# Forming the mixing's sums and differences in PSUM, with the softmax sums on ScalarE

## The chip, the core and the metric

The kernel runs on one core of a Trainium2 chip. The metric is the time of one launch on the device, in microseconds (us). A core has engines that each work through a queue of their own, in order: TensorE (PE in the profile, PEld its weight loads), VectorE (DVE), ScalarE (ACT), GpSimd (POOL) and SyncE (SP, which here only issues DMAs). TensorE writes into PSUM, eight banks of 512 fp32 columns on 128 partitions; VectorE and ScalarE read from there. Engines wait for one another through semaphores.

## The reference

Attention in two forms, the sum of which is mixed by a Fourier transform over positions and channels, and then goes through a feed-forward network. All is fp32; 8 batches, 8 heads, 576 positions, head size 64, 512 channels, 2048 hidden.

```python
out_d  = sm_attn(mean4(q), mean4(k), mean4(v))          # pooled by 4 positions
out_up = np.repeat(out_d, 4, axis=2)
scores = np.where(abs(i - j) < 4, scale * q @ k.T, -1e9)  # local, 7 positions wide
attn   = np.exp(scores - max); attn = attn / (np.sum(attn, axis=-1) + 1e-09)
x      = merge_heads(out_up + attn @ v)
...
mixed  = np.real(np.fft.fft(np.fft.fft(x, axis=1), axis=2))
u      = x + mixed
un     = (u - mean(u)) / np.sqrt(var(u) + 1e-06)
return u + np.maximum(un @ w_ch1, 0.0) @ w_ch2
```

## The kernel before

**Stages.** The work of the 8 batches runs in a pipeline. Up to about 270 us it is attention and mixing; the feed-forward network's first matmuls stand at about 271 us, the last mixing at about 320, and from 560 us on the network runs in a form with fewer products (`Super`). The weights arrive as 64-bit words and are decoded on the way (`Quarter`: ScalarE, GpSimd, three steps on VectorE, then a high and a low part).

**Attention.** A `Unit` is one of 40 spans of 128 positions of a batch: loads of q and k (`load`) and of v with a column of ones (`load_v`), `sum_in` (sums for the pooled attention), `scores`, `maxima`, `exps`, `transpose_p`, `copy_p`, `values`, `result`. Since v has a column of ones, the product `values` leaves the softmax sum in column D of PSUM. `result` (line 808) adds 1e-9 to these sums on VectorE into `rs` (line 817), takes the reciprocal and multiplies. `Pooled` does the same for the pooled attention of a batch in three groups (`result`, lines 651 to 665, with `rsd`).

**Mixing.** `Mix` transforms a batch. VectorE and GpSimd form sums and differences that use the symmetries (`cross`, `channels`, `fold`), TensorE multiplies over positions (`sequence`, `sequence_z`), and then over channels, in slots: two of 128 rows for each batch, and a third of 68 rows for each second batch, 20 in all. For a slot, `mix(t, 0)` forms the even part in one PSUM bank: a product with signs (L945) and two fp32 products with the channel table `chan` (L949), 256 columns each. ScalarE copies it to SBUF (`even_out`, L956), which frees the bank. `mix(t, 1)` forms the odd part in another bank, with two more products of L949. `unfold(t, 0)` and `unfold(t, 1)` (L968) are VectorE instructions that write even + odd and even - odd, interleaving two halves of 256 columns, into the tile `o` (or `ends` for the 68-row slots). Then the bank is given back, and SyncE stores `o` to `um` in DRAM (`store_mixed`), from where the network's blocks load it.

**Order.** Nothing reorders at run time. `at()` gives each step a place from the table `TURNS`, one number for each call of each step, and the steps are emitted in the order of these places, so that one table sets the order on all engines and queues, and with it which PSUM bank a step gets. Where the table has no entry, a step goes by a time in the plan (most of `Super`). The small constant `bits` (identity and mask in bf16) is loaded first on SyncE's queue (line 507); the larger constants come by GpSimd's queue (`constants`, lines 845 to 847).

Of the kernel before, what the change touches and what calls it, by code (L numbers as in the profile page):

```python
# [8 lines left out]
F32 = mybir.dt.float32  # L9
# [18 lines left out]
        49, 124, 252, 388, 530, 652, 781, 917,  # L28
    ),
    "Pooled.copy_v": (  # L30
        51, 131, 256, 395, 535, 659, 789, 918,
    ),
    "Pooled.scores": (
        38, 30, 33, 138, 95, 104, 270, 210, 229, 394, 347, 367, 539, 489, 505, 672, 604, 605, 786, 749, 759,
        937, 864, 890,
    ),
    "Pooled.maxima": (
        54, 32, 36, 149, 98, 110, 275, 212, 234, 402, 356, 382, 545, 495, 511, 675, 608, 614, 796, 751, 761,
        945, 873, 895,
    ),  # L40
    "Pooled.exps": (
        64, 37, 44, 154, 107, 125, 280, 215, 242, 418, 372, 393, 552, 504, 531, 688, 613, 629, 797, 757, 773,
        950, 878, 914,
    ),
    "Pooled.transpose_p": (
        83, 39, 61, 179, 117, 135, 303, 224, 274, 424, 381, 408, 555, 521, 544, 707, 623, 681, 814, 763, 793,
        953, 881, 923,
    ),
    "Pooled.copy_p": (
        85, 41, 66, 183, 122, 146, 308, 233, 279, 437, 386, 413, 569, 529, 558, 718, 634, 683, 819, 768, 811,  # L50
        955, 886, 936,
    ),
    "Pooled.values": (
        92, 53, 80, 192, 132, 153, 312, 267, 287, 439, 403, 425, 581, 540, 559, 720, 668, 694, 837, 804, 822,
        957, 925, 949,
    ),
    "Pooled.result": (
        94, 59, 86, 193, 137, 160, 317, 269, 293, 449, 409, 430, 591, 546, 570, 722, 674, 705, 843, 815, 825,
        963, 939, 951,
    ),  # L60
    "Pooled.store": (
        88, 251, 328, 522, 656, 770, 938, 968,
    ),
    "Pooled.pack": (
        112, 209, 345, 462, 601, 726, 869, 975,
    ),
    "Mix.cross": (
# [3 lines left out]
    ),  # L71
    "Mix.channels": (
# [4 lines left out]
    ),  # L77
    "Mix.fold": (
# [4 lines left out]
    ),  # L83
    "Mix.split_z": (
        99, 141, 194, 254, 349, 377, 501, 499, 577, 654, 710, 798, 852, 909, 987, 999,
    ),
    "Mix.sequence_z": (
        159, 316, 433, 513, 702, 824, 964, 1029,
    ),
    "Mix.z_high": (  # L90
        173, 335, 447, 518, 711, 829, 981, 1034,
    ),
    "Mix.z_low": (
        199, 337, 463, 528, 714, 836, 1000, 1098,
    ),
    "Mix.sequence": (
        216, 200, 175, 181, 338, 336, 332, 319, 476, 483, 458, 459, 573, 578, 600, 599, 762, 745, 742, 736,
        875, 876, 847, 854, 1001, 1007, 990, 995, 1052, 1045, 1071, 1081,
    ),
    "Mix.sequence_out": (  # L100
        228, 190, 344, 342, 488, 469, 588, 606, 764, 747, 885, 855, 1021, 1008, 1066, 1108,
    ),
    "Mix.mix": (
        257, 307, 243, 311, 401, 419, 354, 359, 366, 450, 502, 498, 516, 571, 626, 648, 609, 642, 677, 682,
# [1617 lines left out]
```

## Time and profile before

| | us |
|---|---|
| median of 3 runs | 1082.76 |
| lowest and highest | 1081.66, 1085.46 |
| the profiled execution | 1078.42 |
| its span, first to last instruction | 1076.6 |
| TensorE busy (matmuls) | 1036.2 |
| VectorE busy | 640.1 |
| ScalarE busy | 389.7 |
| GpSimd busy | 328.7 |

The profile is of one execution. Busy time is the time in which at least one instruction of an engine runs. Matmuls are pipelined: one of 512 columns lasts some 0.39 us in the rows, while the next starts 0.23 us after it, so that an uninterrupted sequence shows as fully busy and a wait shows a little shorter than it is. Each fp32 product appears as two passes, and so two rows, of the same line; the one-pass form of the network's products (fp32r) as one. In a row of the timeline or of the groups, `banks<-chan,yf` means that tile `banks` is written from `chan` and `yf`, and brackets or the last field name the idle time of the engine before the instruction, and who ended it. Rows of waits give who waited for whom, the total in us, the number of times and the longest. The busy table by stretches gives, for each, the length, then busy us and instructions of PE, PEld, DVE, ACT and POOL, then the granted clock of TensorE as a share of full speed, the DMA share and GB/s.

### The profile page before, as it was taken

The numbers are of one execution on the slowest core, as the hardware profiler recorded it, in microseconds if no ns is written. First come the engines' busy times: TensorE is split into PE (matmuls) and PEld (weight loads), VectorE is DVE, ScalarE is ACT, GpSimd is POOL, SyncE is SP. The second block draws the span as 40 slices with busy tenths as digits, with TensorE's granted clock in tenths as the row PEclk, the third lists the DMA queues.
The fourth block names the chain that finished last, engine by engine and source line by source line (L and its number), as shares of the span: only waits on it lengthen the run. The fifth ranks groups of instructions, "written<-read, shape, count | busy, mean of one in ns | idle before, by whom it ended". The sixth has DMA issues, their size and how long they took to land.

```text
span 1076.6 us, 21807 instructions
## 1 busy us (share of the span) xinstructions
PE 1036.2 (96%) x8296; PEld 831.4 (77%) x8296; DVE 640.1 (59%) x1226; ACT 389.7 (36%) x1069; POOL 328.7 (31%) x486
## 2 busy tenths in 40 slices
PE   6899999999999999989998999999999999999998
PEld 4677767777877788878886888887788887888886
DVE  6999979889997884354354333564334465333332
ACT  6775667664443442122241111252111143111121
POOL 1222223224654556464641121253212033200000
PEclk9999999999999999999999999999999999999999
DMA  9567768865745554865836787946978643953242
GB/s 349 185 233 237 239 180 243 253 177 172 201 127 180 153 147 133 190 190 163 196 137 175 227 229 204 281 115 170 272 232 224 199 136 89 247 184 136 78 127 78
DMA packets 114400, 201.61 MB, mean 187 GB/s; under 512 B 13792, under 2 KB 30080, under 8 KB 114168
## 3 DMA queue, kind: packets, MB, share of 16 engines
q1 hardware_dynamic: 99752, 173.08, 48.4%
q0 software_dynamic: 14544, 27.15, 14.6%
q8 instruction: 65, 1.06, 0.4%
q14 instruction: 39, 0.32, 0.1%
HBM read 143.22 MB, written 56.43 MB: 185 GB/s over the span
## 4 chain that ended last, share of the span: by engine, by line
PE 71%; DVE 10%; DMA 9%; issue 4%; POOL 3%; SPq 1%; ACT 1%; DVEq 0%; ACTq 0%; POOLq 0%
PE banks L1348 20%; PE banks L1211 11%; PE banks L1209 11%; PE banks L1210 11%; PE banks L1189 9%; PE banks L909 3%; DMA qkT<-in_qk_dram 2%; DMA raw<-in_wq_dram 2%; DVE wt L478 1%; PE banks L1162 1%; PE banks L949 1%; DMA ux<-xb 1%; DMA ut<-um 1%; PE banks L800 1%; DMA um<-o 1%
## 5 line engine op out<-in xcount | busy, mean ns | idle before, releaser
L1209 PE MATMUL banks<-w2h,hh 128*128 128x512 f32 x576 | 228.5, 397 | 0.0
L1211 PE MATMUL banks<-w2h,hl 128*128 128x512 f32 x576 | 225.8, 392 | 2.0 <-DVE hl L1197 1.9
L1210 PE MATMUL banks<-w2l,hh 128*128 128x512 f32 x576 | 225.2, 391 | 0.0
L1193 ACT ACTIVATE hh<-row 128x512 fp32r<-128x512 f32 x72 | 45.6, 633 | 290.1 <-DVE row L1375 173.2
L1348 PE MATMUL banks<-w,w 128*128 128x512 f32 x576 | 144.9, 395 | 4.0 <-ACT raw L1368 4.0
L1189 PE MATMUL banks<-unT,w 128*128 128x512 f32 x576 | 138.2, 392 | 1.1 <-DVE ut L1214 1.1
L1348 PEld LDWEIGHTS banks<-w,w 128*128 128x128 f32 x576 | 109.0, 190 | 28.7 <-ACT raw L1368 4.9
L1211 PEld LDWEIGHTS banks<-w2h,hl 128*128 128x128 f32 x576 | 108.1, 188 | 27.0 <-DVE hl L1197 3.3
L1189 PEld LDWEIGHTS banks<-unT,w 128*128 128x128 f32 x576 | 107.9, 188 | 24.8 <-DVE ut L1214 1.5
L1210 PEld LDWEIGHTS banks<-w2l,hh 128*128 128x128 f32 x576 | 108.2, 188 | 22.6
L1209 PEld LDWEIGHTS banks<-w2h,hh 128*128 128x128 f32 x576 | 108.3, 188 | 22.5
L1197 DVE SCALAR_TENSOR_TENSOR hl<-row,hh 128x512 fp32r<-128x512 f32 x72 | 50.4, 700 | 114.7 <-ACT hh L1193 114.2
L1348 PE MATMUL banks<-unT,w 128*128 128x512 f32 x432 | 106.2, 390 | 2.4 <-DVE w L1375 2.4
L1348 PEld LDWEIGHTS banks<-unT,w 128*128 128x128 f32 x432 | 80.8, 188 | 20.5 <-DVE w L1375 3.7
L1375 DVE TENSOR_TENSOR w<-raw,banks 128x512 f32<-128x512 f32 x48 | 33.0, 688 | 66.2 <-PE banks L1348 64.4
L1197 DVE SCALAR_TENSOR_TENSOR hl<-banks,hh 128x512 fp32r<-128x512 f32 x48 | 32.9, 686 | 65.3 <-ACT hh L1193 62.6
L759 ACT ACTIVATE sb<-banks,mx 128x64 f32<-128x64 f32 x320 | 69.8, 329 | 3.1 <-PE banks L772 1.8
L909 PE MATMUL banks<-seq,f 128*128 128x290 f32 x256 | 67.2, 411 | 2.1 <-DVE xb L820 2.1
L1193 ACT ACTIVATE hh<-banks 128x512 fp32r<-128x512 f32 x48 | 28.5, 594 | 106.9 <-PE banks L1210 73.6
L1147 POOL TENSOR_TENSOR rstd<-rstd,mhalf 128x1 f32<-128x1 f32 x36 | 23.8, 662 | 124.6 <-DVE rstd L1146 124.6
L909 PEld LDWEIGHTS banks<-seq,f 128*128 128x128 f32 x256 | 47.1, 190 | 15.0 <-DVE xb L820 2.2
L1315 POOL TENSOR_TENSOR raw<-raw 128x256 f32<-128x256 f32 x48 | 39.5, 824 | 52.8 <-ACT raw L1268 47.5
(131 smaller groups left out, 1557.2 us busy)
## 6 DMA issues: line engine op xcount, KB each, us to landing
w<-ut SPq DMA_DIRECT2D x96, 256.0 KB
qkT<-in_qk_dram SPq DMA_DIRECT2D x40, 512.0 KB
w<-ub SPq DMA_DIRECT2D x72, 256.0 KB
raw<-in_wq_dram SPq DMA_DIRECT2D x64, 256.0 KB
uh<-w SPq DMA_DIRECT2D x42, 256.0 KB
vaug<-in_vw_dram SPq DMA_DIRECT2D x40, 260.0 KB
out_dram<-ut SPq DMA_DIRECT2D x36, 256.0 KB
um<-o SPq DMA_DIRECT2D x16, 512.0 KB
```

The source lines that it names most:

```text
L759: nc.scalar.activation(out=self.sb[:, hp, z], in_=self.sc[:, z, hp], func=AF.Exp, scale=0.125, bias=self.mx[:, z, hp : hp + 1],)
L909: nc.tensor.matmul(y, l, r, start=(i == 0), stop=(i == len(mms) - 1))
L1147: nc.gpsimd.tensor_tensor(out=rstd, in0=rstd, in1=mhalf, op=ALU.pow)
L1189: nc.tensor.matmul(hps, a[:, c, :], unT[:, x, c, :], start=(i == 0), stop=(i == len(mms) - 1))
L1193: nc.scalar.activation(out=hh, in_=self.hps[f], func=AF.Relu)
L1197: nc.vector.scalar_tensor_tensor(out=hl, in0=self.hps[f], scalar=0.0, in1=self.hh[f].bitcast(F32), op0=ALU.max, op1=ALU.subtract)
L1209: nc.tensor.matmul(acc, hh, w2h, start=start, stop=False)
L1210: nc.tensor.matmul(acc, hh, w2l, start=False, stop=False)
L1211: nc.tensor.matmul(acc, hl, w2h, start=False, stop=stop)
L1315: nc.gpsimd.tensor_tensor(out=out, in0=a, in1=b, op=op)
L1348: nc.tensor.matmul(self.ps[into], w[:, y, c, :], both[z][:, c, :], start=(start and i == 0), stop=(i == len(mms) - 1), skip_group_check=True)
L1375: nc.vector.tensor_add(out=out, in0=raws[a], in1=self.ps[x])
```

## The change

- **Mixing.** A slot has one bank. `mix(t, 0)` forms signs, even and odd products all in it, which gives even + odd. `unfold(t, 0)` copies it out on ScalarE, with the interleaving. `mix(t, 1)` then adds two more products with tables that hold minus twice the odd ones, into the same bank, which gives even - odd, and `unfold(t, 1)` copies that out and gives the bank back. `even_out` and its tile are gone. The table `chan` has six parts in place of four.
- **Softmax sums.** The addition of 1e-9 (4e-9 in the pooled attention) is a step of its own, `total`, an activation on ScalarE with a bias from the small tile `little`; `result` starts with the reciprocal.
- **Constants.** `bits` is loaded by ScalarE's queue.
- **Places.** `TURNS` has new numbers for every step (1999 steps with a place, 1955 before).

```diff
-        49, 124, 252, 388, 530, 652, 781, 917,
+        55, 124, 259, 401, 546, 672, 814, 952,
...
+    little = res.tile([P, 2], F32, name="little")
+    for i, x in enumerate((1e-9, 4e-9)):
+        nc.vector.memset(little[:, i : i + 1], x)
...
-    nc.sync.dma_start(out=bits.bitcast(F32), in_=c_bits)
+    nc.scalar.dma_start(out=bits.bitcast(F32), in_=c_bits)
...
+        def total(self, g):
+            rs = self.rs[g] = pd.tile([P, 2, 2], F32, name="rsd", bufs=2)[:, :, : self.tiles(g)]
+            nc.scalar.activation(out=rs, in_=self.av[g][:, :, :, D], func=AF.Identity, bias=little[:, 1:])
+
         def result(self, g):
-            av, k = self.av[g], self.tiles(g)
-            rs = pd.tile([P, 2, 2], F32, name="rsd", bufs=2)[:, :, :k]
-            nc.vector.tensor_scalar_add(out=rs, in0=av[:, :, :, D], scalar1=4e-9)
+            av, k, rs = self.av[g], self.tiles(g), self.rs[g]
             nc.vector.reciprocal(out=rs, in_=rs)
...
+        def total(self):
+            self.rs = p2.tile([P, 2, HP], F32, name="rs", bufs=2)
+            nc.scalar.activation(out=self.rs, in_=self.av[:, :, :, D], func=AF.Identity, bias=little[:, :1])
...
-            rs = p2.tile([P, 2, HP], F32, name="rs")
-            nc.vector.tensor_scalar_add(out=rs, in0=self.av[:, :, :, D], scalar1=1e-9)
+            rs = self.rs
             nc.vector.reciprocal(out=rs, in_=rs)
...
-    chanm = pf.tile([P, 4, HN], F32, name="chan")
+    chanm = pf.tile([P, 6, HN], F32, name="chan")
...
-        def mix(self, t, odd):
+        def mix(self, t, minus):
 
             cols = self.kept(t)
-            ps = self.ps[t, odd] = bank((self, t, odd), "mix", P if t < 2 else 2 * TAIL)[:, 0]
-            if not odd:
+            if not minus:
+                ps = self.ps[t] = bank((self, t), "mix", P if t < 2 else 2 * TAIL)[:, 0]
                 sg = signs.unsqueeze(2).to_broadcast([P, 2, HD])
                 to = ps.rearrange("p (two n) -> p two n", two=2)
                 nc.tensor.matmul(to, yz[:, cols], sg, start=True, stop=False, skip_group_check=True)
-
-            for half, T in enumerate((3, 1) if odd else (0, 2)):
+                parts = [(0, 0, 0), (1, 2, 2), (0, 3, 3), (1, 1, 1)]
+            else:
+                ps = self.ps[t]
+                parts = [(0, 3, 4), (1, 1, 5)]
+            for half, T, way in parts:
                 to = ps[:, half * HD : (half + 1) * HD]
                 nc.tensor.matmul(
-                    to, self.yh[:, T, cols], chanm[:, T, :], start=bool(odd), stop=True, skip_group_check=True
+                    to, self.yh[:, T, cols], chanm[:, way, :], start=False, stop=way > 2 or way == 1, skip_group_check=True
                 )
-
-        def even_out(self, t):
-            ps = self.ps[t, 0]
-            self.even[t] = pf.tile([P, DM], F32, name="even", bufs=2)[: ps.shape[0]]
-            nc.scalar.copy(out=self.even[t], in_=ps)
-            done((self, t, 0), "mix")
...
-            even, ps = (x.rearrange("p (two n) -> p n two", two=2) for x in (self.even[t], ps))
-            nc.vector.tensor_tensor(
-                out=o.rearrange("p (n two) -> p n two", two=2),
-                in0=even,
-                in1=ps,
-                op=ALU.subtract if minus else ALU.add,
+            nc.scalar.copy(
+                out=o.rearrange("p (n two) -> p n two", two=2), in_=ps.rearrange("p (two n) -> p n two", two=2)
             )
-            if len(self.mixed.setdefault(t, [])) == 1:
-                done((self, t, 1), "mix")
-            self.mixed[t].append(minus)
+            if minus:
+                done((self, t), "mix")
...
-    chan = np.stack([cos[:, 0::2], sin[:, 1::2], cos[:, 1::2], sin[:, 0::2]], axis=1)
+    chan = [cos[:, 0::2], sin[:, 1::2], cos[:, 1::2], sin[:, 0::2]]
+    chan = np.stack([*chan, -2 * chan[3], -2 * chan[1]], axis=1)
```

TensorE's order at the first mixing of a batch, before (L945 and L949 are the mixing's products with `signs` and `chan`, L740 scores, L567 and L642 pooled v and values, L593 and L623 pooled scores and transposes):

```order
L740 MATMUL banks<-qkT 64x64 x16
L567 MATMUL banks<-vaug,poolm 32x260 x8
L567 MATMUL banks<-vaug,poolm 64x260 x2
L945 MATMUL banks<-signs,yz 128x512
L949 MATMUL banks<-chan,yf 128x256 x2
L642 MATMUL banks<-vsum,ptd 64x65 x16
L593 MATMUL banks<-sums 32x160 x8
L623 MATMUL banks<-ident,sd 128x128 x6
```

The same place in the changed kernel (L958 and L965 are the mixing's products, L750 scores, L649 pooled values, L630 pooled transposes, L782 transposes):

```order
L750 MATMUL banks<-qkT 64x64 x16
L649 MATMUL banks<-vsum,ptd 64x65 x16
L958 MATMUL banks<-signs,yz 128x512
L965 MATMUL banks<-chan,yf 128x256 x6
L630 MATMUL banks<-ident,sd 128x128 x6
L965 MATMUL banks<-chan,yf 128x256 x2
L782 MATMUL banks<-ident,sb 128x128 x4
```

The six products of L965 are the first four of slot 0 and the second pair of slot 1, whose first four stand further up; slot 0's second pair follows the six transposes.

ScalarE's order at the mixing's first copies, before (L956 copies an even part, L755 and L759 are a unit's scaling and exps, L604 and L607 the pooled ones, L572 and L573 copy the pooled v):

```order
L607 ACTIVATE sd<-banks,mxd 128x5x32
L956 COPY even<-banks 128x512
L755 ACTIVATE mx<-mx 128x8
L759 ACTIVATE sb<-banks,mx 128x64 x8
L572 COPY vsum<-banks 128x520
L573 COPY vsum<-banks 128x260
L956 COPY even<-banks 128x512
```

And in the changed kernel (L977 copies out a sum or a difference, L660 adds to the pooled softmax sums, L765 and L769 are a unit's scaling and exps, L499 rounds a weight):

```order
L579 COPY vsum<-banks 128x520
L580 COPY vsum<-banks 128x260
L499 CAST w_156<-wt 128x256
L977 COPY o_1547<-banks 128x512
L765 ACTIVATE mx<-mx 128x8
L769 ACTIVATE sb<-banks,mx 128x64 x8
L660 ACTIVATE rsd<-banks,little 128x4
L977 COPY o_1547<-banks 128x512
L977 COPY o_1573<-banks 128x512
```

The first L977 is slot 1's sum, the second slot 0's, behind a unit's exps and a softmax sum, the third slot 1's difference.

SyncE's first DMAs, before (`vaug` is v, `qkT` is q and k, `raw` weights):

```order
L507 DMA bits<-in_c_bits_dram 128x96
L711 DMA vaug<-in_vw_dram 128x520 x2
L707 DMA qkT<-in_qk_dram 128x1024 x5
L711 DMA vaug<-in_vw_dram 128x520
L707 DMA qkT<-in_qk_dram 128x1024 x2
```

And in the changed kernel:

```order
L717 DMA qkT<-in_qk_dram 128x1024 x5
L721 DMA vaug<-in_vw_dram 128x520 x2
L717 DMA qkT<-in_qk_dram 128x1024
L721 DMA vaug<-in_vw_dram 128x520 x3
L717 DMA qkT<-in_qk_dram 128x1024 x3
```

`bits` has moved to the head of ScalarE's queue, and five loads of q and k stand ahead of the first v.

## Rows read from the trace of the kernel before

**Rows 1.** The profile's page: busy us, share and instructions of each engine

```profile
PE 1036.2 (96%) x8296; PEld 831.4 (77%) x8296; DVE 640.1 (59%) x1226; ACT 389.7 (36%) x1069; POOL 328.7 (31%) x486
```

**Rows 2.** Busy time by stretches: length, PE, PEld, DVE, ACT, POOL, clock, DMA

```profile
0.00:60.00 60.00, 46.33 (x1140) 35.30 (x1141) 47.83 (x97) 41.23 (x155) 12.12 (x31) 1.00 0.75 268
60.00:270.00 210.00, 201.75 (x3665) 152.52 (x3664) 190.30 (x426) 136.83 (x470) 60.31 (x105) 0.99 0.70 215
270.00:360.00 90.00, 85.18 (x374) 67.41 (x373) 77.19 (x154) 37.84 (x93) 51.14 (x82) 1.00 0.59 168
360.00:450.00 90.00, 90.00 (x398) 74.53 (x398) 55.59 (x100) 26.76 (x66) 51.69 (x75) 1.00 0.56 152
450.00:560.00 110.00, 106.91 (x492) 87.71 (x492) 50.69 (x86) 29.85 (x69) 57.80 (x78) 1.00 0.64 177
```

**Rows 3.** Who waited for whom, 0 to 60 us: total us, times, longest

```profile
PE banks L740 <- DMA qkT<-in_qk_dram: 3.1, 2, 2.5
...
PE banks L800 <- DVE odt L660: 2.5, 2, 2.3
...
PE banks L593 <- DVE odt L660: 1.4, 1, 1.4
...
PE banks L593 <- DVE rs L817: 0.9, 1, 0.9
```

**Rows 4.** The same, 60 to 270 us

```profile
PE banks L593 <- DVE xb L820: 2.1, 1, 2.1
PE banks L909 <- DVE xb L820: 2.1, 1, 2.1
...
PE banks L642 <- DVE yz L931: 0.5, 1, 0.5
```

**Rows 5.** The same, 270 to 360 us, and last 360 to 560 us

```profile
PE banks L1211 <- DVE hl L1197: 1.9, 2, 1.2
...
PE banks L949 <- DVE hl L1197: 0.7, 1, 0.7
...
PE banks L1162 <- DVE hl L1197: 3.1, 1, 3.1
```

**Rows 6.** Timeline of VectorE: start, us, instruction, idle before and who ended it

```profile
154.17 1.22 DVE L723 TENSOR_REDUCE sums<-qkT 128x256 f32<-128x1024 f32 x1 [3.18 <-DMA qkT<-in_qk_dram]
...
223.70 0.69 DVE L820 TENSOR_TENSOR xb<-banks,rs 128x512 f32<-128x512 f32 x1 [2.29 <-DMA ud<-rest]
...
462.03 3.15 DVE L1069 TENSOR_TENSOR raw<-w 128x512 f32<-128x512 f32 x2 [2.38 <-POOL wt L1079]
```

**Rows 7.** The chain that ended last, 340 to 357 us: start, us, what

```profile
337.18 4.62 DMA raw<-in_wq_dram
```

**Rows 8.** Groups by line: shapes, count, busy us, mean ns, idle before

```profile
L949 PE MATMUL banks<-chan,yf 128*128 128x256 f32 (+1 forms) x160 | 42.2, 390 | 0.7 <-DVE hl L1197 0.7
...
L968 DVE TENSOR_TENSOR o<-even,banks 128x512 f32<-128x512 f32 x32 | 21.5, 694 | 0.2
...
L956 ACT COPY even<-banks 128x512 f32<-128x512 f32 (+1 forms) x20 | 12.0, 598 | 7.8 <-PE banks L949 7.8
...
L755 ACT ACTIVATE mx<-mx 128x8 f32<-128x8 f32 x40 | 8.9, 223 | 19.2 <-DVE mx L752 18.9
...
L817 DVE TENSOR_SCALAR rs<-banks 128x8 f32<-128x8 f32 x40 | 6.3, 158 | 2.1 <-PE banks L800 1.9
...
L968 DVE TENSOR_TENSOR ends<-even,banks 68x512 f32<-68x512 f32 x8 | 5.2, 684 | 0.0
```

**Rows 9.** Timeline of ScalarE's first exps, TensorE's pooled transposes and channel products

```profile
9.26 1.75 ACT L759 ACTIVATE sb<-banks,mx 128x64 f32<-128x64 f32 x8
...
18.80 0.87 PE L623 MATMUL banks<-ident,sd 128*128 128x128 f32 x6 [0.34 <-ACT sd L607]
...
68.60 1.03 PE L949 MATMUL banks<-chan,yf 128*128 128x256 f32 x4
```

**Rows 10.** Timeline of TensorE at the start

```profile
7.07 1.13 PE L740 MATMUL banks<-qkT 64*64 64x64 f32 x32 [2.53 <-DMA qkT<-in_qk_dram]
```

More of the change, by code (lines that the diff above doesn't have):

```diff
@@ L52 @@
+        995, 929, 971,
     ),
     "Pooled.values": (
-        92, 53, 80, 192, 132, 153, 312, 267, 287, 439, 403, 425, 581, 540, 559, 720, 668, 694, 837, 804, 822,
-        957, 925, 949,
+        96, 59, 74, 210, 142, 175, 343, 270, 305, 484, 422, 441, 616, 564, 584, 752, 686, 720, 874, 827, 850,
+        1005, 964, 978,
+    ),
+    "Pooled.total": (
+        105, 64, 82, 211, 150, 178, 345, 280, 313, 487, 423, 444, 618, 581, 588, 755, 697, 730, 880, 843,
+        855, 1013, 972, 990,
     ),
@@ L116 @@
+        820, 833, 832, 853, 985, 1002, 965, 993, 946, 958, 1091, 1127, 1077, 1134, 1179, 1289, 1183, 1213,
+        1155, 1171,
     ),
     "Mix.store_mixed": (
-        357, 436, 624, 828, 904, 1058, 1152, 1267,
+        311, 440, 585, 750, 943, 1040, 1158, 1317,
     ),
     "Mix.store_local": (
-        115, 184, 273, 292, 389, 380, 512, 572, 671, 667, 784, 865, 922, 961, 996, 1004,
+        112, 219, 263, 314, 417, 408, 548, 597, 698, 741, 845, 861, 966, 948, 1051, 1055,
     ),
     "Mix.store_ends": (
-        562, 831, 1199, 1306,
+        473, 937, 1123, 1277,
@@ L157 @@
     ),
     "Unit.values": (
[L159 to L160 removed]
+        39, 78, 65, 87, 101, 131, 168, 201, 218, 241, 297, 319, 344, 358, 361, 437, 460, 489, 501, 508, 663,
+        605, 621, 633, 651, 740, 753, 786, 763, 776, 851, 883, 907, 932, 896, 984, 1017, 1027, 1011, 1037,
+    ),
+    "Unit.total": (
+        41, 89, 68, 99, 108, 136, 169, 204, 224, 247, 301, 320, 349, 360, 363, 438, 477, 494, 509, 512, 671,
+        611, 625, 644, 653, 747, 754, 787, 770, 781, 862, 885, 910, 934, 904, 992, 1034, 1029, 1015, 1045,
@@ L549, in __init__ @@
             self.b = b
-            self.sp, self.mx, self.tp, self.pt, self.av, self.rest = {}, {}, {}, {}, {}, None
+            self.sp, self.mx, self.tp, self.pt, self.av, self.rs, self.rest = {}, {}, {}, {}, {}, {}, None
         def pool_v(self):
@@ L689, in plan @@
             at(self.copy_v)
-            stages = [self.scores, self.maxima, self.exps, self.transpose_p, self.copy_p, self.values, self.result]
+            stages = [self.scores, self.maxima, self.exps, self.transpose_p, self.copy_p]
+            stages += [self.values, self.total, self.result]
             for g in (2, 0, 1):
@@ L829, in plan @@
                 *(self.load, self.sum_in, self.load_v, self.scores, self.maxima, self.exps),
-                *(self.transpose_p, self.copy_p, self.values, self.result),
+                *(self.transpose_p, self.copy_p, self.values, self.total, self.result),
             ):
@@ L853, in __init__ @@
             self.b, self.y = b, {}
-            self.w, self.ps, self.o, self.even, self.mixed = {}, {}, {}, {}, {}
+            self.w, self.ps, self.o = {}, {}, {}
             self.f = self.yh = self.ends = None
@@ L1021, in plan @@
             for slot in range(2 + self.b % 2):
-                at(self.mix, slot, 0)
-                at(self.even_out, slot)
-                at(self.mix, slot, 1)
                 for minus in range(2):
+                    at(self.mix, slot, minus)
                     at(self.unfold, slot, minus)
```

169 lines of the change are left out of this document (80 added, 89 removed), and 102 rows, old and new, of the table TURNS.

## The prediction

> **What bounds the kernel now.** I read the busy shares first. TensorE (PE) is busy for 96% of the span, VectorE (DVE) for 59%, ScalarE (ACT) for 36% [rows 1]. These averages hide two regimes, so I read the stretches next [rows 2]; look at PE and DVE side by side. From 360 to 450 us PE is busy for all 90 us, with 398 matmuls, 226 ns each, while DVE works 55.6 us: there PE alone sets the pace. From 60 to 270 us, where attention and mixing run, PE is busy for 201.75 of 210 us and DVE for 190.30: both are close to full. Work that goes from DVE to PE then pays only as far as PE's idle time is DVE's doing, so that idle time is the whole budget. Before 560 us it is 13.7 + 8.3 + 4.8 + 0 + 3.1 = 29.8 us, the length less PE's busy time in the five rows of [rows 2]. After 560 us the change touches nothing but places.
>
> Who ended those idle times is read from the waits [rows 3 to 5]. I sort them by what DVE itself was doing. In 0:60, 4.8 us are waits for DVE (2.5 + 1.4 + 0.9) and 3.1 for the first q and k loads [rows 3]. In 60:270 seven rows name DVE, from 2.1 down to 0.5 us, together 8.2 [rows 4]; but the two longest, 2.1 us each, aren't DVE's load: DVE had itself idled 3.18 us for a load and 2.29 us for a store [rows 6]. 4.0 us remain. In 270:360 all 4.7 us name DVE, in four rows from 1.9 down to 0.7 [rows 5]. About half, 2.3 us, stand behind transfers of raw weights that pace the decoding on DVE, such as the 4.62 us at 337 [rows 7]; 2.4 us remain. The 3.1 us of [rows 5] at 467 us follow a DVE that had waited 2.38 us for GpSimd (POOL) [rows 6]. So 4.8 + 3.1 + 4.0 + 2.4 = 14.3 us are within reach of lighter DVE queues and an earlier first load, 2.1 + 2.1 + 2.3 + 3.1 = 9.6 us were begun by transfers and POOL, and 5.9 us are the rest.
>
> **The change, part by part: PE.** The profile counts two passes for each fp32 product: L949 has 160 for 20 slots with four products each [rows 8]. The changed kernel has six for each slot, so 20 x 2 x 2 = 80 more passes. Four such passes start and end within 1.03 us, and one lasts 0.39 [rows 8, 9], so starts are (1.03 - 0.39) / 3 = 0.213 us apart. All have 256 moving columns, those of the 68-row slots too. The cost is 80 x 0.213 = 17 us. The signs product L945 stays as it is, and mixing goes on breaking PE's order twice for each slot. Nothing is taken off PE, and nothing can hide these passes except PE's own idle time.
>
> **DVE.** Removed are 40 combinations (21.5 + 5.2 us) and 64 additions to the softmax sums (158 ns each, 10.1 us) [rows 8], together 36.8 us; two memsets come in. Most, some 28 us, falls between 60 and 270 us, where attention runs and three quarters of the combinations stand. DVE then needs some 162 us where PE needs over 200: it is no longer PE's equal.
>
> **ACT.** Removed are 20 copies of even parts, 12.0 us [rows 8]. Added are 40 copies that interleave. ACT's price for the interleaved read isn't in the trace; between the plain copy, 598 ns, and DVE's combination with that pattern, 694 ns [rows 8], I take 0.6, the same engine's: 24 us, at most 28. The 64 sums are small ACT instructions; nearest is the scaling of the maxima, 223 ns for 128x8 [rows 8]: 14.3 us, bounds 13 and 20. Net +26 us. ACT's 136.8 of 210 us in 60:270 [rows 2] rise to some 156, three quarters. It is not full, but at that load others queue behind it.
>
> **The waits that come in.** Two are new. First, the second pair of products writes into the bank that the first copy reads, so PE must wait for that copy, and all that stands behind on PE waits too, scores and values of later units included. How thin the cover can be shows at the first such place in the order: between slot 0's first four products and its second pair, PE has slot 1's second pair (0.85 us) and six transposes (0.87 us [rows 9]); ACT has a scaling, eight exps, a sum and the copy, 0.22 + 1.75 + 0.22 + 0.6 = 2.8 us [rows 8, 9]. If both arrive together, PE waits 2.8 - 1.7 = 1.1 us. Of the other 19 slots, read in the same way, four or so have so little cover; the rest have scores, values or pooled products between. Second, each softmax sum goes PE, ACT, DVE and no longer PE, DVE. That costs PE nothing while banks are free: it holds a bank some 0.2 us longer, against the one bank that each slot of the mixing gives back.
>
> **Start and constants.** The small constant goes to ACT's queue; ACT's first exps stand at 9.26 us [rows 9], so its issue costs nothing there. On SyncE's queue (SP) five q and k loads now come first, where the constant and two loads of v did. The first product with q and k stands at 7.07 us behind its load [rows 10]. An earlier landing can give back between nothing (all transfers behind it still have to pass) and the 3.1 us of [rows 3]. Later on SP, the mixing's stores wait for ACT's copy in place of DVE's combination, and the q and k loads behind them with them. The larger channel table is one POOL DMA as before, long ahead of its first use at 68 us [rows 9].
>
> **The sum.** +17 us of PE work. Of the 14.3 us within reach I take three quarters, 10.7 us: where DVE is at 62% of a stretch (360:450) PE never waits, where it is at 86% (270:360) PE idles for 5% of it [rows 2], and DVE will stand at some 75%, between the two. The 9.6 us begun by transfers I leave. 17 - 10.7 = +6.3 us. The profiled execution took 1078.4 us, so its like would take 1084.7; the median of the three runs is 1082.8, so I predict 1082.8 + 6.3 = **1089 us**. For this kernel a difference under 0.3%, 3.25 us, can't be told from none.
>
> **A rule against this reading.** Between 60 and 270 us the weight loads are busy for 152.52 of 210 us, 73%; from 360 to 450, where PE is surely full, 74.53 of 90, 83% [rows 2]. The Trainium skill (Perfetto Trace Analysis, "Identifying the Most-Contended Engine") says that the busy share of matmuls is no good measure of how near TensorE is to its limit, and that the busy share of its weight loads is a better one. By that rule PE would have a tenth of those 210 us free, some 20 us, the added passes would cost next to nothing, and the relief alone would give 1082.8 - 10.7 = 1072. The idle times of the matmuls, 8.3 us there, don't bear that out, so it has part of the chance of the faster rival and no more.
>
> **Rivals.** *Faster, 1076.* The new places also move the loads and stores that began the long waits, and PE, no longer held by DVE, runs without those gaps: 14.3 + 9.6 = 23.9 us come back, 17 - 23.9 = -6.9 us. For it: 360:450 shows that PE can run so. Against it: it needs four fifths of PE's idle time before 560 us, and a wait for a transfer doesn't end because DVE is lighter. *The same, 1083.* All of the 14.3 and a third of the 9.6 come back: 17.5 against 17. For it: the order is written anew for the new loads. Against it: all engines share one order, and ACT is now fuller. *Slower by more, 1097.* ACT takes DVE's place as the engine that PE waits for: five thin covers at 1.1 us are 5.5 us, and a quarter of the relief, 2.7 us, is lost where sums stand behind exps: 6.3 + 5.5 + 2.7 = +14.5. It decides from the point at which ACT comes to a copy over 1.7 us after PE has finished the products it reads.
>
> **How the numbers follow.** The forecast around 1089 (1086 to 1093): 0.33. Slower by more, 1093 to 1102: 0.14. The same, 1079.5 to 1086: 0.26. Faster, below 1079.5: 0.27. So faster by over 0.3% has 0.27, within 0.3% 0.26, slower by over 0.3% 0.47. As the cases lie on both sides, the forecast's own range is 1086 to 1093; the range meant to hold the time 8 times in 10 goes from 1074 to 1098 and leaves out a full return of all waits and the worst of the ACT rival.
>
> **What would show it.** The channel products as 240 passes, their starts still 0.213 us apart, and PE's busy time up by some 17 us: that is the certain term. DVE's busy time in the first 270 us down by over 30 us. PE's idle time before 560 us at 18 to 20 us: that is the relief; near 6 us means the faster rival, near 28 the slower one. Waits of PE for the interleaving copy, by name, would show ACT's part. The first q and k product before 7.07 us would show the start. I am wrong if the added passes lie beside other work, so that PE's busy time hardly grows, or if the idle time after 560 us, which I carry over unchanged, moves by more than 3 us.

## The result and the profile after

| | before | changed |
|---|---|---|
| median, us | 1084.11 (4 runs) | 1096.38 (4 runs) |
| lowest and highest, us | 1081.66, 1085.64 | 1094.48, 1099.13 |
| profiled execution, us | 1078.42 | 1099.13 |
| its mean granted clock of TensorE | 0.997 | 0.986 |

The changed kernel is slower by 1.24% (ratio 1.0124, 95% interval 1.0098 to 1.0150), some 13 us. The forecast was 1089 and its range reached to 1098, so the sign and the range held, and the point is 7 us too low. The granted clock doesn't explain the difference: at a mean clock of 0.994 the changed kernel took 1094.48 us, and the kernel before, in the experiments below, 1079.7 to 1084.6. The two profiled executions lie below all timed runs of before and at the top of the changed kernel's, so the traces show a difference of 20.7 us, 8 us more than the medians.

The busy line of the page, against [rows 1]: TensorE +23.5 us, VectorE -39.9, ScalarE +23.1.

```profile
PE 1059.7 (97%) x8376; PEld 852.4 (78%) x8376; DVE 600.2 (55%) x1124; ACT 412.8 (38%) x1153; POOL 330.3 (30%) x486
```

The stretches of [rows 2] for the changed kernel (length, then busy us of PE, PEld, DVE, ACT, POOL, then clock, DMA share, GB/s):

```profile
0.00:60.00 60.00, 52.36 (x1198) 40.30 (x1199) 47.30 (x89) 46.87 (x181) 11.69 (x30) 0.94 0.80 287
60.00:270.00 210.00, 201.66 (x3625) 154.00 (x3625) 155.96 (x320) 148.00 (x515) 54.17 (x96) 0.98 0.66 200
270.00:360.00 90.00, 83.69 (x369) 65.44 (x366) 70.48 (x140) 38.20 (x91) 50.97 (x81) 0.98 0.63 174
360.00:450.00 90.00, 89.09 (x394) 73.47 (x393) 57.29 (x112) 28.53 (x71) 44.45 (x70) 1.00 0.55 155
450.00:560.00 110.00, 106.94 (x469) 87.52 (x468) 41.82 (x80) 23.44 (x53) 63.88 (x87) 0.97 0.61 156
```

Read PE and DVE side by side. DVE works 203.3 us in the first 270 us, where it worked 238.1. Part of these 35 us is only that the changed kernel is less far at 270 us: up to the network's first product after attention, at 274.94 us before and now at 291.07, DVE works 242.2 and 220.2 us, 22 us less. PE's idle time before 560 us is 7.6 + 8.3 + 6.3 + 0.9 + 3.1 = 26.2 us, where it was 29.8. Up to the first product of `Super`, which is the same work in both, the stretches are (before, then changed):

```profile
0.00:562.20 562.20, 532.36 (x6072) 419.25 (x6073) 422.06 (x860) 274.70 (x857) 234.75 (x373) 1.00 0.65 195
0.00:581.40 581.40, 555.14 (x6153) 438.47 (x6154) 382.11 (x756) 297.36 (x939) 236.30 (x373) 0.98 0.64 189
```

PE idles 29.8 us there before and 26.3 now (length less busy time), while DVE is 40 us lighter. Ten times as much was lifted off DVE as PE idles less.

Who is waited for has changed, though. Summed over all rows of TensorE's waits in these two stretches, waits for DVE fell from 21.7 to 12.2 us, by 9.5, and all others rose from 7.4 to 13.1, by 5.7: for transfers from 3.4 to 5.9, for ScalarE from 2.7 to 4.5, the rest from 1.3 to 2.7. Waits of TensorE from 60 to 270 us, against [rows 4]:

```profile
PE banks L574 <- DMA vaug<-in_vw_dram: 4.5, 1, 4.5
...
PE banks L810 <- DVE rs L831: 0.9, 1, 0.9
...
PE banks L922 <- DVE xb L833: 0.3, 1, 0.3
```

And from 270 to 360 us, against [rows 5]:

```profile
PE banks L965 <- ACT ends L977: 3.1, 1, 3.1
PE banks L1165 <- DVE un L1157: 1.3, 2, 0.9
PE banks L1214 <- DVE hl L1200: 0.9, 1, 0.9
```

From 60 to 270 us the waits for `xb` on DVE are 0.3 us, where they were 4.2, and one for `ends` on DVE is gone, which before had been:

```profile
PE banks L623 <- DVE ends L968: 1.3, 1, 1.3
```

In their place stand one wait of 4.5 us for a load of v and one of 3.1 us for a copy on ScalarE. In both cases what TensorE waits for stands behind other work in a queue. TensorE at the first of them (start, us, instruction, idle before):

```profile
233.97 1.10 PE L574 MATMUL banks<-vaug,poolm 128*32 128x260 f32 x12
239.58 2.15 PE L574 MATMUL banks<-vaug,poolm 128*32 128x260 f32 x8 [4.51 <-DMA vaug<-in_vw_dram]
```

SyncE at the same time:

```profile
228.96 0.90 SPq L987 DMA_DIRECT2D um<-o  x2
229.95 2.73 SPq L721 DMA_DIRECT2D vaug<-in_vw_dram  x1
232.77 5.42 SPq L1006 DMA_DIRECT2D ux<-xb  x4
```

The load stands behind the mixing's stores on SyncE's queue and is issued over 229.95 to 232.68, with more stores behind it; PE has come to the product that reads it by about 235. At the second, ScalarE has a weight ahead of the copy, and the weight's transfer is late:

```profile
297.69 1.07 ACT L469 ACTIVATE wt<-raw 128x256 f32<-128x256 f32 x3 [7.73 <-DMA raw<-in_wq_dram]
298.67 0.57 ACT L977 COPY ends<-banks 68x512 f32<-68x512 f32 x1
```

The groups of the edit, against [rows 8] (shapes, count, busy us, mean ns, idle before):

```profile
L965 PE MATMUL banks<-chan,yf 128*128 128x256 f32 (+1 forms) x240 | 60.0, 391 | 3.1 <-ACT ends L977 3.1
L977 ACT COPY o<-banks 128x512 f32<-128x512 f32 x32 | 18.8, 597 | 5.4 <-PE banks L965 5.3
```

The channel products are 240 passes and 17.8 us longer than the 42.2 of L949; the interleaving copy takes 597 ns.

### The profile page after: what moved, and what is told of

Same layout as the page of the kernel before. It is cut to its first block, busy times and chain, and to the rows that moved or that the text cites. A ratio compares the mean times of both kernels' runs of the same rounds, so it can differ in the third digit from the quotient of the medians.

```text
span 1097.4 us, 21962 instructions
## 1 busy us (share of the span) xinstructions
PE 1059.7 (97%) x8376; PEld 852.4 (78%) x8376; DVE 600.2 (55%) x1124; ACT 412.8 (38%) x1153; POOL 330.3 (30%) x486
## 5 line engine op out<-in xcount | busy, mean ns | idle before, releaser
L1351 PEld LDWEIGHTS banks<-unT,w 128*128 128x128 f32 x432 | 81.2, 188 | 22.8 <-DVE w L1378 6.0
L769 ACT ACTIVATE sb<-banks,mx 128x64 f32<-128x64 f32 x320 | 69.8, 329 | 1.3
L965 PE MATMUL banks<-chan,yf 128*128 128x256 f32 (+1 forms) x240 | 60.0, 391 | 3.1 <-ACT ends L977 3.1
L1150 POOL TENSOR_TENSOR rstd<-rstd,mhalf 128x1 f32<-128x1 f32 x36 | 23.5, 654 | 115.6 <-DVE rstd L1149 115.4
```

The lines of the kernel that those rows point to most:

```text
L769: nc.scalar.activation(out=self.sb[:, hp, z], in_=self.sc[:, z, hp], func=AF.Exp, scale=0.125, bias=self.mx[:, z, hp : hp + 1],)
L965: nc.tensor.matmul(to, self.yh[:, T, cols], chanm[:, way, :], start=False, stop=way > 2 or way == 1, skip_group_check=True)
L1150: nc.gpsimd.tensor_tensor(out=rstd, in0=rstd, in1=mhalf, op=ALU.pow)
L1351: nc.tensor.matmul(self.ps[into], w[:, y, c, :], both[z][:, c, :], start=(start and i == 0), stop=(i == len(mms) - 1), skip_group_check=True)
```

## The experiments

Ratios are to the kernel before, run on the same chip alongside, with 95% intervals. 0.1% is 1.1 us.

| run | what it is | median us | ratio |
|---|---|---|---|
| before_more | before, odd products twice | 1095.42 | 1.0096 [1.0057, 1.0134] |
| no_second | changed, without the second pair | 1085.65 | 1.0036 [1.0005, 1.0066] |
| short_second | changed, second pair of 32 columns | 1092.97 | 1.0085 [1.0051, 1.0118] |
| both_early | changed, the two long waits moved | 1096.25 | 1.0107 [1.0062, 1.0151] |
| before_light | before, DVE's combinations cut short | 1081.08 | 0.9981 [0.9962, 1.0001] |
| no_second_light | no_second, ACT's copies cut short | 1089.32 | 1.0051 [1.0031, 1.0071] |
| before_sums | before, softmax sums on ACT | 1103.44 | 1.0181 [1.0157, 1.0206] |
| sums_back | changed, sums back on DVE | 1094.77 | 1.0094 [1.0059, 1.0128] |
| sums_dve | changed, sums on DVE at ACT's places | 1100.11 | 1.0138 [1.0107, 1.0168] |
| no_second_sums_back | no_second, sums back on DVE | 1085.51 | 1.0014 [0.9993, 1.0034] |
| old_work_new_places | before's work at the new places | 1099.63 | 1.0146 [1.0126, 1.0167] |
| before_start | before with the new start | 1083.37 | 0.9997 [0.9977, 1.0018] |

In the first four expectations, theory A lays the loss on the added passes, and theory B on the two long waits above; the later ones say what their letters mean.

### What the added passes cost

The passes alone, in the order of before:

```diff
+            for again in range(1 + odd):
-                    to, self.yh[:, T, cols], chanm[:, T, :], start=bool(odd), stop=True, skip_group_check=True
+                    to, self.yh[:, T, cols], chanm[:, T, :], start=bool(odd and not again), stop=True, skip_group_check=True
```

> The kernel before with each odd product made twice (the odd part comes out doubled): 80 passes more at unchanged places, with no relief of VectorE and no new wait. Theory A: nearly the whole 17 us, 1098 to 1101. Theory B: TensorE's idle time of some 30 us before 560 us takes up half, 1090 to 1094.

The changed kernel without them:

```diff
-                parts = [(0, 3, 4), (1, 1, 5)]
+                parts = []
```

> The changed kernel with the second pair of products left out, so the 80 added passes of TensorE and its waits for the first copy are gone (both copies then write the sum, the difference is missing). Theory A, the added passes are what makes the changed kernel slower: 80 x 0.213 = 17 us less than its 1096, so 1079, and TensorE's busy time down by as much. Theory B, the passes lie mostly in idle time of TensorE and the loss is in two places of the new order (TensorE waits 4.5 us for a load of v at 240 us and 3.1 us for a copy at 299 us): only the wait for the copy goes, with its slow clock some 5 us, and a few us of passes, so 1087 to 1090.

And with passes of 32 in place of 256 columns:

```diff
+                n = 32 if minus else HD
-                to = ps[:, half * HD : (half + 1) * HD]
+                to = ps[:, half * HD : half * HD + n]
```

> The changed kernel with the second pair of products cut from 256 to 32 columns (the difference is right in these alone). The wait for the first copy and the order stay; a pass should fall from 0.213 us to the 0.109 us at which 128-column transposes follow one another, 80 x 0.104 = 8 us. Theory A: 1088. Theory B: 1092 to 1096, since the waits stay.

Added to before, the passes cost 0.96%, 10.4 us; taken from the changed kernel, together with the wait for the first copy, they give back 1.24 - 0.36 = 0.88%, 9.5 us. Both times lie between what the theories expected. The two opposite experiments agree, although each has an interval of some 4 us to either side: of 17 us of work about 10 are time. Where the other 7 went, the traces show for the changed kernel only. Up to the first product of `Super` (before_more, then no_second; before and changed stand above):

```profile
0.00:576.20 576.20, 547.93 (x6152) 433.50 (x6153) 424.04 (x860) 275.30 (x857) 234.44 (x373) 1.00 0.64 190
0.00:569.90 569.90, 536.91 (x6073) 423.69 (x6074) 380.39 (x756) 296.18 (x939) 236.61 (x373) 0.99 0.65 193
```

In the changed kernel the passes add 18.2 us to PE's busy time and 11.5 us to the length; its idle time falls from 33.0 to 26.3 us. In before's order they add 15.6 and 14.0 us, and the idle time falls only from 29.8 to 28.3. So there the saving rests on the ratio alone, and its interval (6 to 15 us for the passes) leaves room for most of the 17. The run with short passes is no finer measure: it takes seven eighths of their columns away and gives back 0.4%, in theory B's range, but its interval overlaps those of both neighbours. What is left without the passes, 0.36% or 3.9 us, is all the rest of the change, and it isn't a gain.

### Moving the two long waits

In the changed kernel, two stores and one copy are given earlier places, away from the load and out from behind the weight:

```diff
     "Mix.store_mixed": (
-        311, 440, 585, 750, 943, 1040, 1158, 1317,
+        311, 440, 585, 750, 870, 1040, 1158, 1317,
     "Mix.store_ends": (
-        473, 937, 1123, 1277,
+        473, 760, 1123, 1277,
     "Mix.unfold": (
...
-        1155, 1171,
+        1149.5, 1171,
```

> The changed kernel with three places altered: two stores of mixed rows that stood ahead of the late load of v on SyncE's queue are issued when their data is ready, and the copy that TensorE waits for at 299 us stands ahead of three weight steps of ScalarE that wait for a transfer. Theory A: no more than the slack of the waits, 1093 to 1096. Theory B: both waits and the slow clock after them go, 4.5 + 3.1 + 3 to 5 us, so 1084 to 1088.

1.0107 against 1.0124: nothing that can be told from none. The stretches tell why. The changed kernel:

```profile
0.00:225.00 225.00, 213.53 (x4204) 164.49 (x4205) 177.17 (x346) 168.65 (x603) 55.09 (x106) 0.98 0.72 234
225.00:310.00 85.00, 76.51 (x774) 57.39 (x774) 51.46 (x114) 41.89 (x128) 34.99 (x55) 0.94 0.65 169
```

With the stores and the copy moved:

```profile
0.00:225.00 225.00, 207.68 (x4076) 159.12 (x4077) 171.80 (x338) 167.31 (x598) 52.28 (x102) 0.98 0.71 230
225.00:310.00 85.00, 81.83 (x921) 62.98 (x920) 60.01 (x130) 44.34 (x134) 37.98 (x60) 1.00 0.70 183
```

From 225 to 310 us the idle time went as intended, 8.5 to 3.2 us. But ahead of 225 us it grew from 11.5 to 17.3, and TensorE now waits there for other loads of v, as it didn't in the changed kernel:

```profile
PE banks L572 <- DMA vaug<-in_vw_dram: 6.1, 2, 3.5
```

By 310 us both have done the same (4978 and 4997 matmuls). Theory B falls: the waits at the two places went, and others of their size came in earlier. Through which of the moved steps, the trace doesn't settle.

### Is VectorE's load what TensorE waits for?

First the relief by itself, in the order of before (GpSimd zeroes the tiles once at the start):

```diff
-                out=o.rearrange("p (n two) -> p n two", two=2),
-                in0=even,
-                in1=ps,
+                out=o.rearrange("p (n two) -> p n two", two=2)[:, :16],
+                in0=even[:, :16],
+                in1=ps[:, :16],
```

> The kernel before, with VectorE's 40 combinations of the mixing cut from 512 to 32 columns (most of the sums and differences are left out and stay zero), at unchanged places on every engine. It takes some 25 of VectorE's 640 us away, and nothing else: TensorE and ScalarE do what they did. Theory A (VectorE's load makes TensorE idle, as the prediction's relief supposes; the changed kernel lost the relief to something else): three quarters of the share of 14.3 us that goes with 25 of 36.8 us, about 7 us, come back: 1075 to 1077, ratio 0.993. Theory C (the idle time is set by the fixed order and by transfers, and a lighter VectorE gives nothing back): 1081 to 1084, ratio 0.998 to 1.001.

Then, in the changed kernel without the second pair, ScalarE's copies cut to 32 columns in the same way:

> The changed kernel without the second pair of products (the differences hold the sum instead), and with ScalarE's 40 copies cut from 512 to 32 columns (most of the output of the mixing is left out and stays zero). TensorE does the work of before, VectorE 37 us less than before, ScalarE some 10 us less than before in place of some 15 us more. With full copies this kernel took 1085.65. Theory B (ScalarE took VectorE's place, and its load ate the relief): 1076 to 1079. Theory C (no engine's load but the order sets the idle time): 1083 to 1086.

VectorE lost 18.5 us (640.1 to 621.5 on the page, less than the 25 expected, since a combination of 32 columns still takes 180 ns). The time fell by 0.19% (interval -0.38 to +0.01), 2.1 us, where theory A had about 7 us for 25. TensorE's waits for DVE up to `Super` fell by 1.8 us, 21.7 to 19.9. So in the order of before, VectorE's load is hardly what makes TensorE idle. Cutting ScalarE's copies gave no gain either (1.0051 beside 1.0036 with full copies), so theory B of this pair falls too.

Where the relief goes can be followed in the two profiled executions (1078.42 and, light, 1079.14 us, so that in this pair nothing is gained at the end). TensorE reaches the network's first matmuls after attention at 271.12 us in the light kernel and at 274.94 in before: at that point 3.8 us are gained. The wait of [rows 5] at 467 us takes the last of them. Before:

```profile
464.00 0.39 PE L1211 MATMUL banks<-w2h,hl 128*128 128x512 f32 x1
467.48 0.66 PE L1162 MATMUL banks<-ident,un 128*128 128x128 f32 x4 [3.09 <-DVE hl L1197]
...
468.20 0.40 PE L1210 MATMUL banks<-w2l,hh 128*128 128x512 f32 x1
468.44 0.40 PE L1211 MATMUL banks<-w2h,hl 128*128 128x512 f32 x1
...
470.75 1.57 PE L1189 MATMUL banks<-unT,w 128*128 128x512 f32 x6
```

The light kernel:

```profile
461.87 0.39 PE L1216 MATMUL banks<-w2h,hl 128*128 128x512 f32 x1
466.03 1.12 PE L1167 MATMUL banks<-ident,un 128*128 128x128 f32 x4 [3.77 <-DVE hl L1202]
...
467.38 0.63 PE L1215 MATMUL banks<-w2l,hh 128*128 128x512 f32 x1
467.80 0.63 PE L1216 MATMUL banks<-w2h,hl 128*128 128x512 f32 x1
...
470.75 1.57 PE L1194 MATMUL banks<-unT,w 128*128 128x512 f32 x6
```

The light kernel comes to this wait 2.1 us earlier, waits 0.7 us longer, and then its matmuls of 512 columns start 0.42 us apart, where before's start 0.23 apart: the granted clock in 460:470 is 0.83, and 1.00 in before. Both reach the next product at 470.75. DVE, which is waited for here, was itself waiting for GpSimd, 2.37 us, as in [rows 6].

Ahead of that, the loads show the same pattern. SyncE's own queue, 60 to 270 us, in before:

```profile
SPq L707 <- PE banks L740: 13.7, 6, 4.2
SPq L711 <- PE banks L800: 9.0, 6, 4.3
SPq L452 <- DVE wt L481: 6.8, 1, 6.8
SPq L673 <- DVE odt L660: 4.3, 1, 4.3
```

Loads of q, k and v wait for the scores and values products that free their buffers. VectorE's longest waits were for those loads (11.2 us for q and k before 280 us, 10.5 in the light kernel). So TensorE sets much of the pace of the loads that VectorE waits for, and that part a lighter VectorE doesn't shorten. It isn't the whole: SyncE also waits for VectorE, and loads stand behind those waits in the same queue. That this loop is why so little came back is argued from the waits and not tested by a run.

### The softmax sums

In the kernel before, at the same places:

```diff
-            nc.vector.tensor_scalar_add(out=rs, in0=self.av[:, :, :, D], scalar1=1e-9)
+            nc.scalar.activation(out=rs, in_=self.av[:, :, :, D], func=AF.Identity, bias=little[:, :1])
```

(and likewise 4e-9 in the pooled attention.)

> The kernel before, with one part of the change alone: 1e-9 is added to the softmax sums on ScalarE, at the place of the VectorE addition that it replaces. VectorE gives up 10 us, ScalarE takes some 14. Theory A: 10 of 36.8 us of relief are 2 to 3 us of gain, 1080, unless the way over ScalarE takes them back. Theory C: no gain; each sum now passes through ScalarE's queue and comes later, 1083 to 1087.

Expected was between a gain of 3 us and a loss of 4; it lost 1.81%, 20 us, the largest effect of the study. VectorE's waits up to 280 us in this run:

```profile
DVE rs L821 <- ACT rs L820: 18.7, 16, 3.5
DVE rsd L658 <- ACT rsd L657: 10.7, 11, 2.4
```

And ScalarE's:

```profile
ACT rs L820 <- PE banks L803: 14.5, 12, 4.8
ACT rsd L657 <- PE banks L645: 8.3, 11, 1.1
```

For 29.4 us VectorE stands at a reciprocal until ScalarE has added, and ScalarE stands 22.8 us at the additions until TensorE has the product, each with all that is queued behind. In before, VectorE had waited 1.9 and 1.2 us for TensorE at the additions. Ten us of work taken off VectorE have become three times as much waiting on it. Part of the 20 us is a lower granted clock, 0.978 to 0.990 in the five runs against 0.990 to 0.997 in the 17 of before beside them. The changed kernel gives the sums places of their own, ahead of the reciprocals, and VectorE's idle time there is 8.1 us for `rs`:

```profile
L831 DVE RECIPROCAL rs<-rs 128x8 f32<-128x8 f32 x40 | 7.9, 197 | 8.1 <-ACT rs L820 7.9
```

Does that still cost? In the changed kernel the edit above was turned round: with the addition directly ahead of its reciprocal (sums_back), at ScalarE's place (sums_dve), and as the first of these without the second pair (no_second_sums_back):

> The changed kernel with one part undone: the additions to the softmax sums are back on VectorE, directly ahead of their reciprocals, as in the kernel before. ScalarE gives up 17.7 us, VectorE takes 10 us. Theory E (the way of each sum over ScalarE is a wait of its own: in the changed kernel VectorE stands idle for 11 us at the reciprocals and ScalarE for 14 us at the sums, and that has eaten the relief): with that way gone some 6 to 10 us come back, 1086 to 1090. Theory C (neither engine's load nor its waits are on the path at the new places; only the added passes cost): 1095 to 1098, or somewhat more, since VectorE has more to do.

> The changed kernel with the additions to the softmax sums on VectorE, but at the places that they have on ScalarE in the changed kernel, which are up to some thirty places ahead of the reciprocals. Theory E: the handing over between two engines is gone, but VectorE now stands and waits for TensorE at the early places, with all that is queued behind: between the run with the sums directly ahead of the reciprocals and the changed kernel, 1088 to 1096. Theory C: 1095 to 1098.

> The changed kernel without the second pair of products (the differences hold the sum instead) and with the softmax sums back on VectorE, directly ahead of their reciprocals: of the change only the copies on ScalarE, the constant and the new places are left; VectorE does 27 us less than before, TensorE the same. Theory E: the relief that the prediction meant shows at last, 1075 to 1080. Theory C: as without the second pair alone (1085.65), 1083 to 1087.

With the sums back, 1.0094 in place of 1.0124, and without the second pair 1.0014 in place of 1.0036: 0.30% and 0.22%, 2 to 3 us in both pairs, and each inside its interval. That is likely the price of the way over ScalarE, but theory E had 6 to 10 us, and it falls. With the sums on VectorE at ScalarE's early places, 1.0138 can't be told from the changed kernel's 1.0124; in that trace VectorE stands 16.4 and 14.9 us at the two additions until TensorE has the product, so that moving the early wait to the other engine doesn't end it.

### The places and the start

The kernel before, with the table of the changed one: each even part's copy at the place of the first copy, both combinations at that of the second, and the constant on ScalarE's queue.

> The work of before (separate even and odd parts, combinations and softmax sums on VectorE, 160 passes) at the places of the changed kernel, with the small constant on ScalarE's queue: the even part's copy stands where the sum's copy stands, both combinations where the difference's copy stands. Theory A and B (the new places are neutral or good): VectorE is as full as before, so 1082 to 1085, at most as slow as the kernel without the second pair, 1085.65. Theory D (the new places cost what the relief gives): the new order with VectorE full again loses the relief on top, 1090 to 1093.

1.46% slower, 16 us: worse than any theory had it, and nearest to theory D. The new places don't suit the old work. One thing that they bring shows in TensorE's waits for loads of v, up to 330 us (before, then this run, then no_second_sums_back at the same places):

```profile
PE banks L567 <- DMA vaug<-in_vw_dram: 0.3, 1, 0.3
PE banks L346 <- DMA vaug<-in_vw_dram: 6.3, 3, 4.2
PE banks L350 <- DMA vaug<-in_vw_dram: 5.7, 2, 4.4
```

In all five traces with the table of before (in before_start but for three loads) this wait is at most 0.3 us, in all nine with the new one 3.8 to 8.1 us, whatever the work. And theory D, that the new places cost what the relief gives, can't be dismissed: at the new places, from the old work to no_second_sums_back, TensorE's waits for DVE up to `Super` fall from 25.5 to 12.3 us, and the time by 1.32%, 14 us. But these two runs differ in more than VectorE's load: in banks, in ScalarE's copies, and in my choice for the steps that the table lacks. How much of the 16 us is the table, and how much that choice, stays open. Against theory D stands sums_back, where 10 us of work went from ScalarE back to VectorE at the new places and nothing was lost. It does show that places and work belong together: in this table the new work without its passes costs 3.9 us, the old work 16.

The start alone, in before:

```diff
-    nc.sync.dma_start(out=bits.bitcast(F32), in_=c_bits)
+    nc.scalar.dma_start(out=bits.bitcast(F32), in_=c_bits)
     "Unit.load": (
-        2, 4, 11, 13, 10, 25, 62, 29, 50, 47,
+        -4, -3, 11, 13, -2, 25, 62, 29, 50, 47,
```

> The kernel before with the start of the changed kernel alone: the small constant on ScalarE's queue, and three loads of q and k ahead of the first two of v on SyncE's queue; all else as before. Theory A (an earlier first load shifts TensorE's whole stream, as the upper end of the prediction's start term has it): the first product with q and k stands at about 5 us in place of 7.07, and some 2 us of that are there at the end, 1080 to 1081.5. Theory C (what is gained ahead of a wait that something else ends is given back at that wait): the first product is as early, but the stage after 270 us begins at most 1 us earlier, and the time is 1082 to 1084.

TensorE at the start of this run, against [rows 10]:

```profile
4.81 0.63 PE L740 MATMUL banks<-qkT 64*64 64x64 f32 x32
...
12.62 1.09 PE L800 MATMUL banks<-vaug,pT 64*64 64x65 f32 x32
```

The first product is 2.3 us earlier, the first values 0.9 (13.48 in before), the network's first product 1.0 (273.90), and the time is the same, as theory C had it. That a wait takes the gain back, which is theory C's reason, isn't shown. What the two traces do show is a lower clock in this stretch, before and then this run:

```profile
10.00:15.00 5.00, 4.36 (x120) 3.28 (x111) 4.97 (x8) 4.93 (x24) 0.30 (x2) 1.00 1.03 408
10.00:15.00 5.00, 3.18 (x76) 2.61 (x73) 3.26 (x6) 2.86 (x13) 0.77 (x3) 0.50 1.02 400
```

The granted clock there is 0.50 in place of 1.00, and its mean over the 12 runs 0.989, over the 17 of before 0.993. So a part of the gain may have gone into the clock.

## Why the prediction was right in its sign and too low

**TensorE's passes: right as work, too dear as time.** 240 passes, and L965 is 17.8 us longer against 17 predicted. "Nothing can hide these passes except PE's own idle time" was right, but the sum charged them in full. The ratios give about 10 us for them.

**The relief: the step that failed.** "Of the 14.3 us within reach I take three quarters, 10.7 us", and "The 9.6 us begun by transfers I leave." TensorE's waits for DVE did fall, by 9.5 us up to `Super`. But the sum booked the relief as time, with every other wait as it was, and the places of the new order at nothing beyond the start. In the changed kernel the other waits rose by 5.7 us, those for loads of v from 0.3 to 4.5, and the trace has 26.2 us of idle time before 560 us, where the prediction wanted 18 to 20, near the 28 that it named for the slower rival. In time, nothing of 10.7 us is left: without the second pair and with the sums back the kernel takes 1.0014 [0.9993, 1.0034] of before. At the old places before_light had half of the relief give 2.1 us, with zero at the edge of its interval.

Why so little is left stays open between two accounts. Either the new places took what the relief gave, for which the loads of v and old_work_new_places speak, or a lighter VectorE gives little in any order, for which before_light and sums_back speak. No run has the whole new work at the old places. In either case the ground for the term was weak. I put waits down as DVE's load wherever DVE hadn't idled just before, and set the share that returns by DVE's busy share in three stretches. These stretches differ in the work, not only in the load: 360:450 has no loads of q, k and v, and no buffers to be freed by scores.

**The sum.** 17 - 10.7 was +6.3; measured by the ratios, it is 10 for the passes, 2 to 3 (not certain) for the sums over ScalarE, and the rest, 1.5 us (0.14%, interval -0.07 to +0.34), for copies, places, start and relief together: 13 to 14. The parts add up because each is a step between two runs, and are no test of one another. The errors went opposite ways: the passes were some 7 us too dear and the relief some 10 too large. That the time stayed inside the range, 1.6 us below its end, is in part luck.

**VectorE and ScalarE.** DVE lost 36.8 us by prediction, 39.9 on the page; the interleaving copy took 597 ns against 0.6 us. The 64 sums went for 275 to 287 ns and not 223, 18 us and inside the bounds. ACT's net is +23.1 against +26.

**The waits that come in.** The thin covers did not show: the only wait for an interleaving copy, 3.1 us at 299, came from a weight's transfer ahead of it on ScalarE. That the sum's way over ScalarE "costs PE nothing while banks are free" was too kind: it costs what is queued behind the waiting engines, little at the new places and 20 us at the old ones.

**The start.** The first q and k product at 4.99 us confirms the step; in before_start it changed the time by nothing that can be told (-0.23% to +0.18%).

**The rivals.** 1097 came nearest in time, but not for its reason: shortening ScalarE's copies and taking its sums away hardly moved the time, so ScalarE's load did not take VectorE's place, though TensorE's waits for it rose by 1.8 us. The rule of the Trainium skill (Perfetto Trace Analysis, "Identifying the Most-Contended Engine") takes the busy share of the weight loads as the better measure of how near TensorE is to its limit; from their 73% I had worked out a tenth of TensorE's time as free. The runs don't decide on it: some 7 of the 17 us found room, but the 29.8 us in which the matmuls idle had room for them too. The 1072 that I worked out from it would have needed all 17, and the relief besides. After 560 us nothing moved by 3 us: from the first product of `Super`, at 562.2 us and now at 581.4, to the end of the span are 514.4 and 516.0 us.

## What to carry to other kernels

An engine that is busy and waited for isn't yet the cause of the waiting: shorten its work in place, leaving its order as it is, before a gain is booked for it; here 18.5 us off VectorE gave 2. A new order brings waits of its own: here 9.5 us fewer for one engine came with 5.7 us more for the others, so book the sum of all waits and not those that go. Extra work on the engine that sets the pace can cost less than its length, here about 10 of 17 us, where a part falls into its waits. A step handed to a third engine in order-bound queues costs the waiting on both sides: 10 us of small additions cost 20 us of time at unchanged places.

## What the runs showed of the hardware

A wait of TensorE can cost more than its length. In the changed kernel, after the 4.5 us of 235 to 239.6, the granted clock is 0.65 between 240 and 246, and the first four channel passes there span 1.98 us, where four took 1.03 [rows 9]:

```profile
234.00:240.00 6.00, 1.49 (x18) 0.54 (x16) 3.27 (x8) 3.77 (x15) 3.76 (x7) 0.78 0.62 180
240.00:246.00 6.00, 6.00 (x24) 3.61 (x21) 0.00 (x0) 1.39 (x4) 2.10 (x4) 0.65 0.96 215
```

PE counts as busy for all of 240:246; at a clock of 0.65 that is the work of some four us. So the busy line overstates TensorE's work: of its +23.5 us, the passes are 17.8. The spacing after the wait of 3.77 us shown above, 0.42 us for 512 columns, is the lower of the clock's two levels, 1.2 GHz, and agrees with the 426.7 ns that the Trainium skill gives for it (TensorE: Matmul & The Clock Gate, "Wait — 56ns, not 53.3ns?"). Not every such wait is followed by it: after the 3.09 us at 467 us the clock stayed at 1.00 in before's trace, and fell to 0.91 in that of before_start at a wait of the same length. So the cost of one wait differs from run to run, and effects of a few us are read from several runs and not from two traces.

The mean granted clock goes with the time of one and the same kernel: of the 19 runs of before beside no_second, the three at 0.983 to 0.987 took 1089.2 to 1090.1 us, the four at 0.996 to 0.998 took 1077.1 to 1083.0. The runs without the second pair, and before_start, stand at 0.989 in the mean, where the runs of before beside them stand at 0.992 to 0.993, so a part of what these kernels lack may be clock. Whether their order brings the lower clock, no run settles.
